# A recurrent attention and gated feed-forward kernel: chunk 0's keys and right side moved ahead of the first inverse, x kept in channel order, weights loaded into five rooms

## The chip, the cores and the metric

The kernel runs on one core of a Trainium2 chip. The metric is the device time of one execution in microseconds (us). The kernel before took 1059.27 us, the median of three runs (1058.33 to 1067.59). The profile is of one more execution, which took 1057.22 us.

The core's engines have their own instruction queues and run in order: TensorE (PE in the profile, its weight loads PEld) multiplies matrices into PSUM; VectorE (DVE), ScalarE (ACT) and GpSimd (POOL) work elementwise; SyncE (SP) only issues DMA transfers, and so does ScalarE at the start. In the profile SPq and ACTq are these issues.

## The reference

Two blocks, one behind the other. The first is a linear recurrence over 768 tokens for 4 batches and 8 heads of 40 channels, with a state of 40 x 40 per head:

```
for t in range(S):
    y[t]  = r[t] @ state
    Sa    = state @ a[t]
    state = state * w[t] - outer(Sa, b[t]) + outer(v[t], k[t])
```

`w` is a decay per channel, between 0.85 and 0.95. The heads of `y` side by side are `x`, 3072 tokens of 320 channels. The second block is a feed-forward layer with 2048 hidden channels:

```
h = x @ w_in
out = (h * sigmoid(h)) @ w_out
```

All inputs are float32 except the weights of the second block, which are float64 and come to the device as pairs of 32-bit words.

## The kernel before

**Chunks.** The sequence is cut into 12 chunks of 64 tokens (index n). A unit (n, m) is one chunk of two of the four batches with all their heads; a chunk has two units. Inside a chunk the recurrence becomes matrix products with a triangular matrix that has to be inverted. Two heads lie on the partitions, 64 apiece, of which 40 are used.

**Preparing a unit** (`pre`, `scale` and `scores`). VectorE scans the decays into their running products `W` (L229) and takes the reciprocal (L238); GpSimd scales `a` (L239) and the keys `kb` (L241). TensorE forms the scores (L209, in `between`), VectorE masks them (L217), and SP writes them to DRAM as `md` (L257). The tile of decays, `w0`, is one buffer; the load of the next unit's decays (`load_w`, L196) waits until the former unit is done with it. Only the first four units have a tile each (`w0` and `early`), loaded on ScalarE's queue.

**Inverting** (`inverse`). For two chunks at a time, 128 triangular blocks of 32 x 32 lie on the 128 partitions (`mi`, read back from `md`, L275). VectorE inverts them in `XI`, column by column, 31 rows of a product and a reduction each (L279, L285). Then `XI` goes to DRAM (`zd`, L292) and also turned (ScalarE's copy into `mi`, L293; `xd`, L294), and is fetched into `XT` (L307, L310). `merge` completes the 64 x 64 inverses with small products (L322, L339).

**The chain of a unit** (`chain`). `keys` transposes the keys (L385); `right` forms the right side from scores (L209, L217), from the carried state `Gbd` (L394) and from the values (L406) and copies it into `RHS`; `solve` applies the inverse (L428, L446); `update` brings the state forward (L466, L475, L479); `read` and `write` form the output (L505, L513, L525, L532, L543) and write it to DRAM as `xs` (L552 to L557); `turn` transposes the state for the next chunk (L488, L497).

**The gated part** (`moe`) takes the 512 tokens of two chunks at a time. `fetch` reads `xs` into `xt` (L569, L571). A part is 16 steps: four `first` (L581, L586, the sigmoid L589 and the product L590 into `gts`), four `second` (L597, L606), then four and four again with the other half of the hidden channels (L597, L609, and the output's transfer L613). `in_order` keeps its matmuls in the order of the program.

**Weights** (`weights`). The float64 weights are loaded in 40 pieces of 128 x 256 numbers, and each is converted to float32 by five VectorE and three ScalarE instructions (L147 to L155). A piece is loaded by up to four transfers (L142) right ahead of its conversion, into a tile that rotates through two or three others (`room`, `xt`, `mi`, `tmp`). `x` is held in an order of its own, three groups of 40 channels and eight more on 128 partitions, so the rows of `w_in` are picked to match.

**The order of work.** The program writes steps in an order made by hand; `weave` merges lists of steps evenly. A planner then orders each engine's queue by its own model of time, with the program's order as priority, so an instruction may run ahead of others that the program has before it, where its data and buffers allow. PSUM tiles named `att` (five) serve the attention, `moe` (three) the gated part. `tc.issue_after(x)` keeps instructions of the same engine behind the instruction x.

The program's order is: load four units, prepare chunk 0; prepare chunk 1, with the first four pieces of weights ahead of the inverse; the inverse; then for each chunk its loads, its chain, and the preparation of the chunk after the next. Pieces 4 to 19 are woven with chunk 0's chain, 20 to 35 with chunk 1's. The preparation of chunks 2 and 3, the second inverse and the last four pieces are woven with the first 12 steps of the first gated part:

```
if n == 1:
    queue = more
    fetch()
    with tc.issue_after(mark["turn"]):
        weave(queue[0:12], ready + held + ahead)
```

From chunk 2 on a chunk's chain is woven with up to eight gated steps; behind an odd chunk the fetch and four steps of the next gated part follow at once, so that an even chunk finds 12 steps in the queue and an odd one four.

A last check counts scan values beyond a limit; if any is, a slow path at the end computes all again. It doesn't run here.

## Time and profile before

| | |
|---|---|
| median of three runs | 1059.27 us |
| profiled execution | 1057.22 us |
| its span, first to last instruction | 1055.4 us |
| mean granted TensorE clock | 0.921 |
| TensorE busy | 847.7 us (80%) |
| VectorE busy | 575.7 us (55%) |
| ScalarE busy | 291.4 us (28%) |
| GpSimd busy | 92.9 us (9%) |
| bytes moved by DMA | 85.37 MB, 81 GB/s in the mean |

Busy time counts an engine's own instructions, not the issue of transfers. A group's row gives line, engine, operation, output and inputs, shapes and count, then busy time, mean duration in ns of one, idle time just before, and what ended it. A row of the timeline gives start, duration, engine, line, operation, output and inputs, count, and in brackets the idle time before it with what ended it. A stretch's row gives start and end, length, busy time and count of the engines named, the granted TensorE clock (1.00 is full), the share of the 16 DMA engines that was busy, and GB/s.

### The profile page before, as it was taken

Reading aid. Unit: us, or ns where it says so; the run is one execution under the profiler, and the core shown is the slowest. Engines: PE = TensorE matmul, PEld = TensorE weight load, DVE = VectorE, ACT = ScalarE, POOL = GpSimd, SP = SyncE. Lnnn points to the kernel's source line nnn. Section 1 sums busy time; section 2 is a strip of 40 time slices with the busy share of each in tenths; the row PEclk is TensorE's granted clock in tenths of the full one; section 3 lists DMA queues with packets and bytes.
Section 4 is the critical chain, followed back from the end, with each engine's and each line's share of the span. In section 5 each row is a group of like instructions: output and inputs, shape, how many; then the busy total and the mean of one; then the engine's idle time right before and its main releaser. Section 6 shows DMA issues by size and latency. Waiting matters only on the chain.

```text
span 1055.4 us, 25618 instructions
## 1 busy us (share of the span) xinstructions
PE 847.7 (80%) x11010; PEld 591.2 (56%) x11010; DVE 575.7 (55%) x1039; ACT 291.4 (28%) x628; POOL 92.9 (9%) x90
## 2 busy tenths in 40 slices
PE   0004899079979768999897999889999899996997
PEld 0003889025359662676663686735667647775444
DVE  8793474766942669525379345398164780412111
ACT  1303462642213321242212233122423023230110
POOL 6101000012000110000100002010001000000000
PEclk9999776579987887999899999989999999998999
DMA  6433353454033543333440343421433403202001
GB/s 155 127 80 80 91 142 95 132 145 97 10 92 82 131 105 56 77 83 85 98 124 12 71 121 88 109 76 44 88 92 78 119 15 69 60 21 56 0 1 28
DMA packets 200424, 85.37 MB, mean 81 GB/s; under 512 B 161648, under 2 KB 191856, under 8 KB 200304
## 3 DMA queue, kind: packets, MB, share of 16 engines
q1 hardware_dynamic: 197584, 83.01, 31.8%
q8 instruction: 88, 1.44, 0.6%
q10 hardware_dynamic: 2720, 0.66, 0.3%
q14 instruction: 32, 0.26, 0.1%
HBM read 66.32 MB, written 17.30 MB: 79 GB/s over the span
## 4 chain that ended last, share of the span: by engine, by line
PE 58%; DVE 24%; DMA 7%; SPq 3%; issue 3%; ACT 3%; POOL 2%; DVEq 0%; POOLq 0%; ACTq 0%
PE po L597 16%; PE ph L581 10%; DVE tmp L279 6%; DVE XI L285 5%; DVE w L238 5%; PE pl L505 4%; PE ph L586 3%; PE pm L209 3%; PE py L525 3%; PE pu L428 3%; PE py L532 3%; PE pt L385 2%; PE po L339 2%; PE pg L466 2%; PE pr L406 2%
## 5 line engine op out<-in xcount | busy, mean ns | idle before, releaser
L581 PE MATMUL ph<-xt,wi_s 128*128 128x512 f32 x384 | 197.4, 649 | 70.0 <-DMA xt<-xs 52.3
L597 PE MATMUL po<-wo_s,gts 128*128 128x320 f32 x768 | 219.9, 442 | 0.0
L597 PEld LDWEIGHTS po<-wo_s,gts 128*128 128x128 f32 x768 | 144.8, 193 | 64.3 <-issue 4.8
L581 PEld LDWEIGHTS ph<-xt,wi_s 128*128 128x128 f32 x384 | 72.4, 203 | 168.8 <-issue 70.3
L590 DVE TENSOR_TENSOR gts<-ph,sg 128x512 f32<-128x512 f32 x96 | 63.6, 683 | 153.5 <-ACT sg L589 153.4
L589 ACT ACTIVATE sg<-ph 128x512 f32<-128x512 f32 x96 | 52.6, 595 | 240.4 <-PE ph L586 240.3
L279 DVE TENSOR_TENSOR tmp<-XI,mi 128x1 f32<-128x1 f32 (+30 forms) x186 | 102.5, 551 | 8.8 <-DMA mi<-md 4.0
L285 DVE TENSOR_REDUCE XI<-tmp 128x1 f32<-128x1 f32 (+30 forms) x186 | 93.2, 501 | 5.2
L209 PE MATMUL pm<-a,kb 64*64 64x64 f32 x1536 | 48.1, 244 | 52.4 <-POOL kb L241 22.2
L322 PE MATMUL pq<-XT,sb 32*32 32x32 f32 x768 | 25.7, 199 | 69.9 <-DMA XT<-zd 69.9
L241 POOL TENSOR_TENSOR kb<-kb,w 128x512 f32<-128x512 f32 x42 | 50.8, 1231 | 320.7 <-DVE w L238 185.6
L209 PEld LDWEIGHTS pm<-a,kb 64*64 64x64 f32 x1536 | 38.8, 151 | 62.3 <-POOL kb L241 39.7
L238 DVE RECIPROCAL w<-W 128x512 f32<-128x512 f32 x21 | 70.3, 3349 | 1.3
L322 PEld LDWEIGHTS pq<-XT,sb 32*32 32x32 f32 x768 | 23.1, 115 | 76.8 <-issue 75.5
L217 DVE TENSOR_TENSOR sk<-pm,ms 128x256 f32<-128x256 f32 x48 | 18.1, 416 | 83.5 <-PE pm L209 83.1
L239 POOL TENSOR_TENSOR a<-a,W 128x512 f32<-128x512 f32 x24 | 28.2, 1178 | 395.2 <-DMA a<-in_aT 261.5
L586 PE MATMUL ph<-xt,wl_s 64*128 64x512 f32 x192 | 61.0, 671 | 0.0
L497 ACT COPY GT<-pt 40x512 f32<-40x512 f32 x44 | 25.5, 579 | 98.0 <-PE pt L488 97.3
L475 DVE TENSOR_TENSOR Gbd<-pg,Gbd 64x320 f32<-64x320 f32 x44 | 21.5, 488 | 52.0 <-PE pg L466 51.2
L543 DVE TENSOR_TENSOR yx<-py,W 64x512 f32<-64x512 f32 x48 | 33.0, 688 | 30.1 <-PE py L532 29.4
L505 PE MATMUL pl<-r,vut 64*128 64x64 f32 x768 | 49.4, 285 | 0.0
L505 PEld LDWEIGHTS pl<-r,vut 64*128 64x128 f32 x768 | 47.8, 200 | 1.7 <-issue 1.2
(98 smaller groups left out, 1023.7 us busy)
## 6 DMA issues: line engine op xcount, KB each, us to landing
a<-in_aT SPq DMA_DIRECT2D x24, 256.0 KB
kb<-in_bT SPq DMA_DIRECT2D x48, 128.0 KB
kb<-in_kT SPq DMA_DIRECT2D x48, 128.0 KB
vut<-in_vT SPq DMA_DIRECT2D x48, 128.0 KB
r<-in_rT SPq DMA_DIRECT2D x24, 256.0 KB
room<-in_w_out SPq DMA_DIRECT2D x20, 256.0 KB
room<-in_w_in SPq DMA_DIRECT2D x48, 80.0 KB
v<-in_v SPq DMA_DIRECT2D x48, 80.0 KB
```

The costliest lines, as they stand in the source:

```text
L209: nc.tensor.matmul(pm[j][C * be : C * be + C, p * C : p * C + C], lhsT=u.kb[J, q, n, :], rhs=u.a[J, q, :], start=True, stop=True,)
L238: nc.vector.reciprocal(R, u.W[:, :, 1 : C + 1])
L241: nc.gpsimd.tensor_tensor(out=u.kb[:, :, n], in0=u.kb[:, :, n], in1=R, op=ALU.mult)
L279: nc.vector.tensor_tensor(out=tmp[:, 0:n, 0:n], in0=XI[:, t + 1 : 32, t + 1 : 32], in1=mi[:, t, t + 1 : 32].unsqueeze(1).to_broadcast([128 ...
L285: last = nc.vector.tensor_reduce(out=XI[:, t + 1 : 32, t], in_=tmp[:, 0:n, 0:n], axis=AX.X, op=ALU.add)
L322: nc.tensor.matmul(pq[be][r + 32 : r + 64, h * 32 : h * 32 + 32], lhsT=s[r : r + 32, h, 32:64], rhs=X[r : r + 32, h, 32:64], start=True, s ...
L505: nc.tensor.matmul(pl[j][:, q * C : q * C + C], lhsT=u.vut[J, q].rearrange("p n t -> p (n t)"), rhs=u.r[J, q, :], start=True, stop=True,)
L581: in_order(nc.tensor.matmul(ph[n], lhsT=wi_s[:, k, at : at + 128], rhs=xt[:, k, :], start=k == 0, stop=False))
L586: in_order(nc.tensor.matmul(ph[n], lhsT=wl_s[R, i, :], rhs=xt[R, 2, :], start=False, stop=True))
L589: nc.scalar.activation(out=sg, in_=ph[n], func=AF.Sigmoid)
L590: nc.vector.tensor_tensor(out=box["gts"][:, (2 * i + n) % (NF // 2), :], in0=ph[n], in1=sg, op=ALU.mult)
L597: in_order(nc.tensor.matmul(po[:, 0:DM], lhsT=box["gts"][:, f, b * 128 : b * 128 + 128], rhs=wo_s[:, NF // 2 * half + f, :], start=f == 0, ...
```

## The change

- Chunk 0's values and queries are loaded with the first units, and its `keys` and `right` stand ahead of the first inverse. In chunk 0 the products with the state, which is zero there (L394 and L525), are left out.
- The first eight pieces of weights are converted between the start of the first inverse and its rows. What follows, the loads of chunk 2 included, is traced behind the last row (VectorE instructions only behind that row). The preparation of chunk 2 moves from there into chunk 1's chain, that of chunk 3 and the second inverse stay with the first gated part.
- The loads of weights are parted from the conversions: five are issued at the start, into four rooms laid in the tile `gts` and one `room`, and each conversion issues the load five pieces on. In the second half there are three rooms (`room`, `mi`, `tmp`) and the load is three pieces on. Pieces 8 to 19 are woven with chunk 0, 20 to 33 with chunk 1, 34 to 39 with the first gated part.
- `x` is held in channel order: `xs` is two writes per unit instead of six, a piece of `w_in` is one transfer (the pieces of the last 64 rows are two).
- A unit's decays are two transfers over all 128 partitions instead of four; the padding's zeros need ones in `one`, and the memset of the whole tile goes.
- The turned copy of `XI` is split between ScalarE and VectorE.
- Gated steps: none with chunks 2 and 3, eight with each chunk from 4 on; none placed behind an odd chunk but the fetch. Four steps of the gated part before are left in the queue ahead of each new one, also at the end.

```diff
     early = [
         sb.tile([128, 32 * 32], F32, name=x)[:, 0 : Q * (C + 1)].rearrange("p (q t) -> p q t", q=Q)
-        for x in ("tmp", "mi", "room")
+        for x in ("tmp", "mi", "xt")
     ]
+    for w in [w0] + early:
+        nc.vector.memset(w[:, :, 0:1], 0.0)
     nc.vector.memset(one, 0.0)
+    for j in range(2):
+        nc.vector.memset(one[DP * j + 32 : DP * j + DP], 1.0)
+        nc.vector.memset(one[DP * j + 32 : DP * j + D], 0.0)
     nc.vector.memset(one[:, :, 0:1], 1.0)
-    for w in [w0] + early:
-        nc.vector.memset(w, 1.0)
-        nc.vector.memset(w[:, :, 0:1], 0.0)
...
+    def load_weights(n):
+
+        if n == 0:
+            rooms["gts"] = sb.tile([128, 4, 4 * WS], I32, name="room4", tag="gts")
+        if n < NW // 2 and n % 5 < 4:
+            rooms[n] = rooms["gts"][:, n % 5]
+        else:
+            tag = "room" if n < NW // 2 else ("room", "mi", "tmp")[n % 3]
+            rooms[n] = sb.tile([128, 4 * WS], I32, name="room", tag=tag)
+        for lo, hi, src in pieces[n][1]:
+            raw = rooms[n][lo:hi, 0 : 2 * WS]
+            nc.sync.dma_start(raw.rearrange("p (i x) -> p i x", x=256) if len(src.shape) == 3 else raw, src)
...
         nc.vector.tensor_tensor(out=dst, in0=f, in1=e, op=ALU.mult)
+        ahead = 5 if n + 5 < NW // 2 else 3
+        if n + ahead < NW and (n + 5 < NW // 2 or n + ahead >= NW // 2):
+            load_weights(n + ahead)
...
         for be in range(2):
-            for j in range(2):
-                J = slice(DP * j, DP * j + D)
-                queue.dma_start(
-                    at[J, P * be : P * be + P, 1 : C + 1],
-                    wT[2 * u.m + be, u.n, J].rearrange("p (q t) -> p q t", q=P),
-                )
+            queue.dma_start(
+                at[:, P * be : P * be + P, 1 : C + 1], wT[2 * u.m + be, u.n].rearrange("p (q t) -> p q t", q=P)
+            )
...
             nc.sync.dma_start(zd, XI)
-            nc.scalar.copy(out=mi, in_=XI.rearrange("p t s -> p s t"))
+            turned = XI.rearrange("p t s -> p s t")
+            nc.scalar.copy(out=mi[:, 0:16], in_=turned[:, 0:16])
+            nc.vector.tensor_copy(out=mi[:, 16:32], in_=turned[:, 16:32])
             nc.sync.dma_start(xd, mi)
...
-            for p in range(P):
+
+            for p in range(P if u.n > 0 else 0):
...
-            for q in range(Q):
+            for q in range(Q if u.n > 0 else 0):
...
             for j in range(2):
                 nc.sync.dma_start(
-                    x[0 : 3 * D, j].rearrange("(p e) t -> e p t", p=3), y[DP * j : DP * j + D, 0:3]
-                )
-                nc.sync.dma_start(x[3 * D : 128, j], y[8 * j : 8 * j + 8, 3])
-            nc.sync.dma_start(x[0:24, 2], y[16:D, 3])
-            nc.sync.dma_start(x[24:64, 2], y[DP : DP + D, 3])
+                    xs[:, at : at + 2 * C].rearrange("(p two e) t -> two e p t", two=2, e=D)[j],
+                    y[DP * j : DP * j + D],
+                )
...
+    for n in range(5):
+        load_weights(n)
+    convert = [partial(weights, n) for n in range(NW)]
+    xs = dr.tile([DM, 4 * NM * C], F32, name="xs", bufs=2)
+    for u in units[0]:
+        load_rv(u)
+    run(prepare(0))
     for t in RHS + Gbd + GT + XT:
         nc.gpsimd.memset(t, 0.0)
...
+    run(prepare(1))
+    chains = {0: [chain(u, xs) for u in units[0]]}
+    run([x[i] for i in range(2) for x in chains[0]])
+    steps = invert(1)
+    run(steps[0:1] + convert[0:8] + steps[1:32])
     queue = []
...
+    with tc.issue_after(mark["row"]):
+        for u in units[2]:
+            load(u)
+        run(steps[32:])
+        steps = [x for pair in zip(*[x[2:] for x in chains[0]]) for x in pair]
+        weave(late.pop(0) + steps, convert[8:20])
+        for u in units[1]:
+            load_rv(u)
+        for u in units[3]:
+            load(u)
+        steps = [x for pair in zip(*[chain(u, xs) for u in units[1]]) for x in pair]
+        weave(steps[0:4], convert[20:24])
+        weave(steps[4:], convert[24:34], prepare(2))
+    fetch, queue = moe(0, xs)
+    fetch()
+    with tc.issue_after(mark["turn"]):
+        weave(queue[0:12], prepare(3) + convert[34:] + invert(3))
+    del queue[0:12]
+    for n in range(2, NN):
...
+        now = 8 if n > 3 else 0
+        weave(steps[0:4], queue[0 : now // 4])
+        weave(steps[4:], queue[now // 4 : now], prepare(n + 2) + invert(n + 2))
+        del queue[0:now]
         if n % 2 == 1:
             fetch, more = moe(n // 2, xs)
...
+            fetch()
+            queue += more
+    run(queue)
```

`prepare(n)` now holds only the preparation, `invert(n)` the inverse and the merges; `run` executes a list of steps. The slow path at the end follows the new order of `x`.

90 lines of the change are left out of this document (24 added, 66 removed).

## The prediction

> **What bounds the kernel now.** I read busy time by stretch first, cut where the chain of waits changes hands, then the timeline at the cuts. Columns: microseconds, length, then PE (TensorE), its weight loads, DVE (VectorE), ACT (ScalarE) and POOL with instruction counts, granted clock, DMA share, GB/s.
>
> ```profile
> span 1055.4 us, 25618 instructions
> ```
>
> ```profile
> 16.00:20.00 4.00, 0.60 (x24) 0.41 (x16) 3.95 (x5) 3.38 (x7) 4.00 (x5) 1.00 0.90 208
> 34.10:46.60 12.50, 0.00 (x0) 0.00 (x0) 7.74 (x17) 4.85 (x13) 0.00 (x0) 1.00 0.51 143
> 46.60:86.50 39.90, 0.00 (x0) 0.00 (x0) 37.97 (x71) 3.56 (x9) 5.75 (x4) 1.00 0.33 83
> 86.50:115.20 28.70, 19.72 (x432) 18.60 (x432) 4.53 (x14) 10.87 (x19) 2.35 (x2) 0.97 0.45 115
> 115.20:184.60 69.40, 64.82 (x1106) 61.44 (x1105) 41.78 (x111) 32.01 (x78) 0.00 (x0) 0.69 0.40 108
> 184.60:214.70 30.10, 1.00 (x35) 0.73 (x32) 23.57 (x76) 18.69 (x46) 0.00 (x0) 0.57 0.51 152
> 214.70:308.30 93.60, 80.86 (x289) 41.08 (x290) 70.87 (x119) 24.99 (x52) 11.65 (x10) 0.94 0.32 78
> 540.60:595.50 54.90, 46.93 (x200) 24.89 (x199) 46.02 (x69) 13.14 (x25) 4.87 (x4) 0.97 0.23 62
> 682.20:738.20 56.00, 50.74 (x259) 28.31 (x258) 49.60 (x81) 12.82 (x24) 4.87 (x4) 0.94 0.22 63
> 974.10:1055.40 81.30, 73.72 (x224) 38.74 (x224) 12.27 (x20) 10.40 (x20) 0.00 (x0) 0.96 0.04 9
> ```
>
> There are two regimes. Up to 86.5 us TensorE waits for the first inverse, and VectorE is the engine at work (37.97 of 39.90). From 308 us on TensorE is fed, with holes in the windows where a later inverse runs (8.0 of 54.9 and 5.3 of 56.0 us idle in the two shown). Between lies the costliest hole, 184.6 to 214.7: one TensorE microsecond in thirty, while VectorE and ScalarE convert weights. The last stretch is one whole gated part, its 16 steps in 73.7 us of TensorE. So a microsecond saved ahead of 308 us is worth about one at the end; later only holes count.
>
> The sum is made against the profiled execution: 1057.2 us, of which 1055.4 are span. The median of the three runs, 1059.3, is 2 us above it.
>
> **Start and first inverse.**
>
> ```profile
> 2.03 3.84 ACTq L196 DMA_DIRECT2D w<-in_wT  x4
> ```
>
> ```profile
> 8.54 1.24 DVE L229 TENSOR_TENSOR_SCAN W<-w,one 128x520 f32<-128x520 f32 x1 [3.57 <-DMA w<-in_wT]
> ```
>
> ```profile
> 32.24 1.23 DVE L229 TENSOR_TENSOR_SCAN W<-w,one 128x520 f32<-128x520 f32 x1
> 33.60 3.35 DVE L238 RECIPROCAL w<-W 128x512 f32<-128x512 f32 x1
> ```
>
> ```profile
> L217 DVE TENSOR_TENSOR sk<-pm,ms 128x256 f32<-128x256 f32 x48 | 18.1, 416 | 83.5 <-PE pm L209 83.1
> ```
>
> VectorE's share of the rows' stretch, 46.5 to 86.5 us:
>
> ```profile
> L279 DVE TENSOR_TENSOR tmp<-XI,mi 128x1 f32<-128x1 f32 (+30 forms) x31 | 16.9, 546 | 0.9
> L285 DVE TENSOR_REDUCE XI<-tmp 128x1 f32<-128x1 f32 (+30 forms) x31 | 15.6, 502 | 1.0
> L238 DVE RECIPROCAL w<-W 128x512 f32<-128x512 f32 x1 | 3.3, 3343 | 0.0
> L229 DVE TENSOR_TENSOR_SCAN W<-w,one 128x520 f32<-128x520 f32 x1 | 1.2, 1230 | 0.0
> ```
>
> Work on the tile room alone (VectorE, ScalarE, POOL):
>
> ```profile
> 115.20:184.60 69.40, 23.20 (x75) 18.20 (x45) 0.00 (x0) 0.69 0.40 108
> 184.60:214.70 30.10, 22.30 (x72) 17.63 (x44) 0.00 (x0) 0.57 0.51 152
> ```
>
> Five VectorE instructions make a piece: 75 are 15 pieces, 1.55 us of VectorE each. Where conversions run alone, 14.4 pieces in 30.1 us, a piece takes 2.1.
>
> (a) The first decay load is two transfers instead of four, and waits for no memset of the whole tile. Four issues took 3.84 us, the scan began 2.7 us behind the last. Two are worth at most 1.9, the memset 1.0. Padding adds bytes while the transfer engines are 0.90 busy, which could take all of it. I take 2: VectorE is done with its four units, and free, near 30 instead of 32.2.
>
> (b) Then come four score masks of chunk 0 (1.7) and eight conversions instead of four: 8 x 1.55 to 2.1, so rows start between 44 and 49. I take 47, no gain: the four extra conversions fill the wait in which VectorE now idles (12.50 less 7.74) and the scan and reciprocal at 32.24, 4.6 us, which leave. Ahead of the score writes the queue now gets, by the shapes in the code, 1.31 MB of weights, 1.66 MB of values and queries, and 0.4 MB of padding: 3.4 MB at 208 GB/s are 16 us, from 20 to 36. The scores, written and read back behind them, then land near 41, hidden by the conversions up to 47. With that cover gone I allow 6 us.
>
> (c) The rows' stretch loses a scan and reciprocal (4.5) and a conversion (1.55): 39.9 becomes 33.8, end near 81. Gain 6.
>
> (d) Behind the rows:
>
> ```profile
> 86.52 1.96 ACT L293 COPY mi<-XI 128x1024 f32<-128x1024 f32 x1 [1.99 <-DVE XI L285]
> ```
>
> ```profile
> 88.09 0.76 SPq L196 DMA_DIRECT2D w<-in_wT  x1
> 88.95 0.44 SPq L292 DMA_DIRECT2D zd<-XI  x1
> ```
>
> ```profile
> 94.37 0.81 PE L322 MATMUL pq<-XT,sb 32*32 32x32 f32 x12 [62.86 <-DMA XT<-zd]
> ```
>
> The first write back waited 2.4 us behind decay loads that aren't there any more, and half of the turned copy goes to VectorE: ScalarE's 1.96 becomes about 1.0. TensorE starts 6 us behind the rows instead of 7.9, at 87 instead of 94.4.
>
> (e) Keys and right side of chunk 0, in TensorE's groups from 94.3 to 115.3 us:
>
> ```profile
> L385 PE MATMUL pt<-ident,kb 128*128 128x128 f32 x16 | 3.7, 424 | 0.0
> L406 PE MATMUL pr<-v,sk 64*64 64x40 f32 x64 | 2.6, 228 | 0.0
> L209 PE MATMUL pm<-a,kb 64*64 64x64 f32 x64 | 2.4, 272 | 0.0
> L394 PE MATMUL pr<-Gbd,a 128*64 128x80 f32 x32 | 2.0, 266 | 0.0
> ```
>
> Of 10.7 us 2.0 are dropped, and 8.7 move to where TensorE is idle. Some overlapped the merge; I take 9. The first solve moves from 115 to 98.
>
> **Chunks 0 and 1** (115.2 to 184.6). TensorE loses half of this group, 5 us:
>
> ```profile
> L525 PE MATMUL py<-r,GT 64*64 64x64 f32 x128 | 10.4, 278 | 2.7 <-DVE Gbd L475 2.6
> ```
>
> VectorE gains: 26 pieces instead of 15 (+17) and the two units of chunk 2 (+9). Loads of five pieces lie ready when the rows end, and from 81 to 98 VectorE has little else (4.53 of 28.70 now), so 8 pieces fall there (-12). 41.8 + 17 + 9 - 12 = 56 us of VectorE stand beside 60 of TensorE, in a chain that alternates between them. I take 66 for 69.4, bounds 60 and 82: end at 164.
>
> **The hole in front of the gated part.**
>
> ```profile
> 164.06 26.00 SPq L142 DMA_DIRECT2D room<-in_w_in  x19
> ```
>
> ```profile
> 202.38 0.36 SPq L552 DMA_DIRECT2D xs<-yx  x1
> ```
>
> ```profile
> 214.72 6.00 PE L581 MATMUL ph<-xt,wi_s 128*128 128x512 f32 x8 [28.90 <-DMA xt<-xs]
> ```
>
> From 164 us SP's queue holds weight loads, each waiting for a room that a conversion must empty, so x, computed by 184, was written at 202. In the changed kernel six pieces come behind chunk 1 instead of twenty, a w_in piece is one transfer instead of four, and x is two writes per unit instead of six. What is left is the round trip; a later one took 8.3 us, from 540.6 to this row:
>
> ```profile
> 548.87 3.70 PE L581 MATMUL ph<-xt,wi_s 128*128 128x512 f32 x8 [2.32 <-DMA xt<-xs]
> ```
>
> I take 12 for 30.1: the gated part starts at 176 instead of 214.7.
>
> **To the merge of chunk 2.**
>
> ```profile
> 239.66 1.23 DVE L229 TENSOR_TENSOR_SCAN W<-w,one 128x520 f32<-128x520 f32 x1
> ```
>
> ```profile
> 285.82 17.61 PE L597 MATMUL po<-wo_s,gts 128*128 128x320 f32 x64
> 308.29 0.92 PE L322 MATMUL pq<-XT,sb 32*32 32x32 f32 x14 [4.86 <-DMA XT<-zd]
> ```
>
> Chunk 3's second unit is scaled 25 us behind the gated part's start; the second inverse follows, and the merge at 308. The 16 gated steps need 74 us, VectorE's share is 70.87, little changed. I take 85 for 93.6: 261 instead of 308. Running sum -47.
>
> **The rest.** Chunk 2 loses its four steps of filler. Just these (17.61 us above) run ahead of the merge now, though the program has them behind it; they can do so again, and I cost it at nothing. If they can't, a rival below has the price. In three later windows the four leftover steps stand in front of the fetch of x and cover it: -4 each. At the end TensorE waits for the last fetch:
>
> ```profile
> 974.08 5.21 PE L581 MATMUL ph<-xt,wi_s 128*128 128x512 f32 x8 [8.69 <-DMA xt<-xs]
> ```
>
> Four leftover steps take that place: -9. Fewer issues on SP, of a third to one microsecond each by the rows above, in chunks 2 and 3: -3. In all -47 - 12 - 9 - 3 = -71; 1057.2 - 71 = 986.
>
> **Rivals.**
>
> The queue holds x again. Loads are now issued right behind a conversion, a round ahead, and so stand even earlier in SP's queue. For it: the row at 164.06. Against: six pieces are left, not twenty. It costs the 18 us from 184 to 202, and some 6 more for chunk 3's decay loads in the same queue: 1010.
>
> Full clock in chunks 0 and 1. If feeding TensorE without gaps lifted 0.69 to the next gated stretch's 0.94, its 60 us would be 44 and VectorE's 56 decide: 10 less, 976. Against: TensorE was busy 93% there, and got 0.69. [...]
>
> No change that can be measured. VectorE's work ahead of the second merge isn't smaller: 186 busy us between 34 and 308 (six rows above), 68%. If waits keep that density, nothing is gained there and the end's 9 us are left: 1048.
>
> Slower: the inverse windows run dry. Now four gated steps and a fetch are placed at the window itself. In the changed kernel none is; all must come forward past the merge. If they can't, a window of 55 us has no matmul, 47 more idle than now, at four windows (behind chunks 3, 5, 7, 9): +188, against -59 from the rest, 1186. It decides from 15 us more per window. Against: 285.82, where four steps did come forward.
>
> Early transfers that crowd the score writes are inside the range, by (b). [...]
>
> **How the numbers follow.** Forecast, 986: 0.62. Queue: 0.16. Full clock: 0.06. No change: 0.08. Dry windows: 0.08. The forecast's own range is 973 to 1009, its bounds added as squares: start (-3, +6), chunks 0 and 1 (-6, +16), the stretch to 308 between 74 and 94 (-11, +9), windows without gain (+12). Below, the range reaches on to the full clock with all lower bounds (976 - 20), above to the queue's 1010 with the windows and the stretch to 308 at their upper ends (+21): 956 to 1031. About 1% is what a measurement of this kernel tells from no change. Faster: 0.62 + 0.16 + 0.06 = 0.84; same 0.08; slower 0.08.
>
> **What would show it.** Rows in one piece of 34 us that ends near 81, with no scan in it; first pq near 87; keys and right side ahead of 50. Chunk 1's last yx near 164, xs and xt directly behind, ph near 176. The next merge's pq near 261. No idle in front of the last gated part. It is wrong if the rows start behind 55, if weight loads stand between yx and xs, or if the windows behind chunks 5 and 7 show over 10 us idle.

## The result, and the profile after

The changed kernel took 979.44 us, the median of four runs (971.43 to 991.06), against 1058.8 for the kernel before beside it: a ratio of 0.922, with a 95% interval of 0.912 to 0.932. In a second group of runs it took 974.74 (972.2 to 976.51), a ratio of 0.915 (0.910 to 0.920). The profile of the first group was of a disturbed execution, so the lines here are from the second, which took 972.2 us. Against the 1057.2 of the profile before these are 85 us less; 71 were forecast.

The stage marks of the two profiles, in us from the start of the span:

| mark | before | forecast | after |
|---|---|---|---|
| first row of the first inverse | 46.6 | 47 | 46.3 |
| last row ends | 86.5 | 81 | 83.5 |
| first pq (merge of chunk 0) | 94.4 | 87 | 89.3 |
| first solve (pu) | 115.2 | 98 | 106.1 |
| last x of chunk 1 computed | 183.5 | 164 | 173.4 |
| first gated matmul (ph) | 214.7 | 176 | 179.4 |
| merge of chunk 2 (pq) | 308.3 | 261 | 265.9 |
| merge of chunk 4 | 443.2 | | 397.7 |
| merge of chunk 6 | 595.4 | | 529.9 |
| last matmul ends | 1047.8 | | 963.0 |

42 us are gained up to the merge of chunk 2 (47 forecast), 42 behind it (24 forecast).

Busy time by stretch of the changed kernel, cut at or near these marks; the columns are those of the prediction's first fence (engines with instruction counts, granted clock, DMA share, GB/s):

```profile
28.00:39.00 11.00, 7.70 (x176) 6.99 (x176) 10.39 (x31) 8.00 (x21) 1.45 (x2) 0.97 0.57 118
39.00:46.30 7.30, 0.00 (x0) 0.00 (x0) 0.02 (x1) 0.24 (x1) 0.00 (x0) 0.50 0.75 181
46.30:83.50 37.20, 0.00 (x0) 0.00 (x0) 35.27 (x78) 5.41 (x14) 0.00 (x0) 0.50 0.49 124
89.30:106.10 16.80, 13.22 (x256) 12.91 (x256) 10.53 (x18) 7.53 (x17) 3.88 (x3) 0.50 0.49 117
106.10:172.70 66.60, 62.84 (x1064) 60.19 (x1063) 50.88 (x119) 34.19 (x87) 3.73 (x3) 0.71 0.53 142
172.70:179.40 6.70, 0.60 (x15) 0.44 (x12) 6.46 (x19) 4.25 (x10) 0.00 (x0) 0.66 0.63 182
179.40:265.90 86.50, 74.62 (x269) 36.96 (x270) 74.33 (x125) 24.93 (x56) 12.14 (x10) 0.91 0.22 57
397.70:529.90 132.20, 127.35 (x1842) 88.59 (x1841) 85.43 (x139) 38.77 (x84) 14.40 (x12) 0.99 0.41 97
```

The keys and right side lie in the first stretch, where TensorE was idle before. The hole ahead of the gated part, 30.1 us long before, is 6.7; counted from the end of the last x it was 31.2 and is 6.0. From the merge of chunk 4 to that of chunk 6 it takes 132.2 us instead of 152.2.

The second line is not what was forecast: ahead of the first row VectorE has nothing to do for 7.3 us. The timeline there (start, duration, engine, line, operation; in brackets the idle time in front and what ended it):

```profile
30.52 9.07 SPq L264 DMA_DIRECT2D md<-sb  x16
39.69 1.27 SPq L204 DMA_DIRECT2D w<-in_wT  x2
41.08 1.23 SPq L282 DMA_DIRECT2D mi<-md  x2
42.36 3.92 SPq L145 DMA_DIRECT2D room<-in_w_in  x6
46.30 0.16 DVE L286 TENSOR_TENSOR tmp<-XI,mi 128x1 f32<-128x1 f32 x1 [7.28 <-DMA mi<-md]
```

Only five of the eight conversions were done at 39, those whose pieces were loaded at the start. SP took 9.07 us to issue 16 writes of the scores, then loaded decays, then read the scores back; the loads of the next pieces stood behind that, at 42.4. So the other three conversions came between the first rows, from 47.2 to 52.3.

The merge of chunk 0, on ScalarE (`qq` is the copy of the first product `pq`, which the second product `po` needs):

```profile
92.19 0.58 ACT L341 COPY qq<-pq 32x512 f32<-32x512 f32 x1
96.82 0.63 ACT L251 ACTIVATE junk<-w 128x512 bf16<-128x512 f32 x1 [4.05 <-DVE w L245]
97.56 0.58 ACT L341 COPY qq<-pq 32x512 f32<-32x512 f32 x1
```

and on TensorE:

```profile
98.19 1.00 PE L348 MATMUL po<-XT,qq 32*32 32x32 f32 x15 [3.46 <-ACT qq L341]
```

Between the two copies that the merge waits for, ScalarE's queue holds a sum of squares of chunk 2's decays, which waits for VectorE's reciprocal of them. So the scaling that the rows got rid of stands in the merge now.

### The profile page after: what moved, and what is told of

It is laid out like the page before. It is cut to its first block, busy times and chain, and to the rows that moved or that the text cites. A ratio compares the mean times of both kernels' runs of the same rounds, so it can differ in the third digit from the quotient of the medians.

```text
span 989.2 us, 25109 instructions
## 1 busy us (share of the span) xinstructions
PE 849.9 (86%) x10914; PEld 597.4 (60%) x10914; DVE 581.3 (59%) x1045; ACT 281.1 (28%) x628; POOL 92.9 (9%) x90
## 5 line engine op out<-in xcount | busy, mean ns | idle before, releaser
L605 PE MATMUL po<-wo_s,gts 128*128 128x320 f32 x768 | 214.5, 436 | 0.0
L589 PEld LDWEIGHTS ph<-xt,wi_s 128*128 128x128 f32 x384 | 70.2, 198 | 124.1 <-issue 65.7
L286 DVE TENSOR_TENSOR tmp<-XI,mi 128x1 f32<-128x1 f32 (+30 forms) x186 | 100.0, 537 | 11.0 <-DMA mi<-md 6.0
L216 PE MATMUL pm<-a,kb 64*64 64x64 f32 x1536 | 45.7, 240 | 39.5 <-POOL kb L248 20.6
L216 PEld LDWEIGHTS pm<-a,kb 64*64 64x64 f32 x1536 | 36.8, 148 | 50.8 <-POOL kb L248 41.0
L515 PE MATMUL pl<-r,vut 64*128 64x64 f32 x768 | 60.6, 310 | 0.0
L515 PEld LDWEIGHTS pl<-r,vut 64*128 64x128 f32 x768 | 58.8, 223 | 1.6 <-issue 0.9
L594 PE MATMUL ph<-xt,wl_s 64*128 64x512 f32 x192 | 58.0, 671 | 0.5 <-DMA xt<-xs 0.5
L485 DVE TENSOR_TENSOR Gbd<-pg,Gbd 64x320 f32<-64x320 f32 x44 | 21.5, 488 | 57.4 <-PE pg L476 56.4
```

The lines of the kernel that those rows point to most:

```text
L216: nc.tensor.matmul(pm[j][C * be : C * be + C, p * C : p * C + C], lhsT=u.kb[J, q, n, :], rhs=u.a[J, q, :], start=True, stop=True,)
L286: nc.vector.tensor_tensor(out=tmp[:, 0:n, 0:n], in0=XI[:, t + 1 : 32, t + 1 : 32], in1=mi[:, t, t + 1 : 32].unsqueeze(1).to_broadcast([128 ...
L515: nc.tensor.matmul(pl[j][:, q * C : q * C + C], lhsT=u.vut[J, q].rearrange("p n t -> p (n t)"), rhs=u.r[J, q, :], start=True, stop=True,)
L589: in_order(nc.tensor.matmul(ph[n], lhsT=wi_s[:, k, at : at + 128], rhs=xt[:, k, :], start=k == 0, stop=False))
L594: in_order(nc.tensor.matmul(ph[n], lhsT=wl_s[R, i, :], rhs=xt[R, 2, :], start=False, stop=True))
L605: in_order(nc.tensor.matmul(po[:, 0:DM], lhsT=box["gts"][:, f, b * 128 : b * 128 + 128], rhs=wo_s[:, NF // 2 * half + f, :], start=f == 0, ...
```

## The experiments

Each is the changed kernel with one edit, unless it says otherwise. They ran in three groups, each beside the kernel before: medians 1063.7 (first four), 1062.3 (next four) and 1057.7 (last four). Across groups the ratios are compared.

**The changed kernel again** (no edit).

> The changed kernel once more, unchanged, for a profile beside the others on one chip. Both theories: 970 to 985 us, second merge's first pq between 262 and 275 us.

Measured: 974.74 us, ratio 0.915 (0.910 to 0.920).

**Only the placement of the gated steps**, put into the kernel before.

```
-            weave(steps[0:4], queue[0:2])
-            weave(steps[4:], queue[2:8], ahead)
-            del queue[0:8]
+            now = 8 if n > 3 else 0
+            weave(steps[0:4], queue[0 : now // 4])
+            weave(steps[4:], queue[now // 4 : now], ahead)
+            del queue[0:now]
...
-                left = max(...)
-                queue[left:left] = [fetch]
+                fetch()
                 queue += more
-                take = len(queue) - 12 if n + 2 < NN else 0
-                weave(queue[0:take])
-                del queue[0:take]
```

> The kernel before with only the new placement of the gated steps (none with chunks 2 and 3, eight with each chunk from 4 on, none behind an odd chunk, four left in the queue). Theory of the prediction, in which this part is worth 12 us in the windows and 9 at the end: 1036 us. Rival, in which the windows are the larger half of the gain: 1015 to 1025 us. Rival of the dry windows: slower than before.

Measured: 1037.4 us (1025.56 to 1044.19), ratio 0.967 (0.958 to 0.977): 26 us less than the kernel before beside it by the medians, 35 by the ratio.

**Only that placement undone** in the changed kernel (the same lines the other way round).

> The changed kernel with the old placement of the gated steps, all else kept. Theory of the prediction: 21 us slower than the changed kernel, about 997 us. Rival (windows are the larger half): 35 us or more slower, 1010 us or above. Dry windows: faster than the changed kernel.

Measured: 1002.04 us (998.94 to 1015.05), ratio 0.944 (0.936 to 0.952): 27 more than the changed kernel by the medians, 31 by the ratios. The two chunks from the merge of chunk 4 on, with the placement undone:

```profile
397.00:544.00 147.00, 137.88 (x1863) 93.59 (x1862) 86.06 (x139) 39.28 (x85) 14.00 (x12) 0.97 0.36 87
```

and those of the kernel before with the new placement:

```profile
446.50:586.60 140.10, 132.58 (x1838) 90.68 (x1838) 86.22 (x138) 40.13 (x84) 13.99 (x12) 0.96 0.38 89
```

132.2 became 147.0; 152.2 became 140.1. Done alone and undone alone, the placement is worth 26 and 27 us by the medians, 35 and 31 by the ratios; the forecast had 21 (three windows of 4 and the end's 9). The windows did not run dry.

**Chunk 0's keys and right side behind the inverse again.**

```
-    run([x[i] for i in range(2) for x in chains[0]])
...
-        steps = [x for pair in zip(*[x[2:] for x in chains[0]]) for x in pair]
-        weave(late.pop(0) + steps, convert[8:20])
+        steps = [x for pair in zip(*chains[0]) for x in pair]
+        steps[4:4] = late.pop(0)
+        weave(steps, convert[8:20])
```

> The changed kernel with chunk 0's keys and right side behind the inverse again (still without the products with the zero state). Theory of the prediction: their 8 us come back onto the path, 984 us. Rival, in which the merge, not they, sets the first solve, as copies on ScalarE leave TensorE time for them: no more than 3 us slower, 979 us.

Measured: 992.86 us (988.4 to 994.49), ratio 0.930 (0.924 to 0.935): 18 more, beyond both expectations. From the first pq to the first solve it takes 24.4 us (87.9 to 112.4) instead of 16.8, close to the 8 expected; as the rows ended 1.5 us earlier, only 6 of the 18 are at the first solve. The others arise in chunks 0 and 1 and in front of the gated part; this run's stretches:

```profile
32.00:87.90 55.90, 0.00 (x0) 0.00 (x0) 45.82 (x114) 11.59 (x28) 0.00 (x0) 1.00 0.41 106
87.90:108.00 20.10, 15.56 (x336) 14.57 (x336) 9.20 (x18) 9.42 (x21) 3.55 (x3) 1.00 0.30 57
112.40:190.00 77.60, 68.42 (x1073) 64.68 (x1072) 50.93 (x125) 36.12 (x91) 3.50 (x3) 0.70 0.52 137
190.00:201.80 11.80, 0.00 (x0) 0.00 (x0) 10.39 (x26) 5.81 (x15) 1.14 (x1) 0.50 0.86 219
```

Chunks 0 and 1 take 77.6 us instead of 66.6 with the same VectorE work (50.93 and 50.88), and the hole is 11.8 instead of 6.7. Which wait makes the 11 us was not tried. The wait of the merge for chunk 2's reciprocal is here as well:

```profile
95.34 0.63 ACT L251 ACTIVATE junk<-w 128x512 bf16<-128x512 f32 x1 [4.04 <-DVE w L245]
```

**Chunk 2's scaling behind the merge.**

```
             for g, J in halves:
-                nc.vector.tensor_tensor(
+                last = nc.vector.tensor_tensor(
                     out=g, in0=g, in1=u.W[J, :, C : C + 1].to_broadcast([DP, Q, D]), op=ALU.mult
                 )
+            if u.n == 0:
+                mark["update"] = last.ins
...
-        weave(steps[4:], convert[24:34], prepare(2))
+        weave(steps[4:], convert[24:34])
+        with tc.issue_after(mark["update"]):
+            run(prepare(2))
```

> The changed kernel, with the scaling of chunk 2's two units (scan, reciprocal, their squares on ScalarE) held back until chunk 0's state update is done. Theory: in the merge of chunk 0 ScalarE waited 4.05 us for chunk 2's reciprocal ahead of the second qq copy, and TensorE waited for that copy 3.5 us; with the scaling behind the merge the first solve starts at 101 to 102.5 instead of 106.1, and the kernel takes 970 to 972 (3 to 5 less), since the 4.6 us of VectorE's scan and reciprocal that leave come back where VectorE has some slack. Rival A: the merge is slow because its matmuls run at half clock; then the first solve stays above 105 and the time at 974 to 976. Rival B: the scaling comes too late for chunk 2, whose scores then hold up the second inverse: first solve at 102, but 980 or more.

Measured: 982.64 us (973.87 to 992.52), ratio 0.925 (0.915 to 0.935): not faster than the changed kernel. The merge, on ScalarE:

```profile
91.92 0.58 ACT L341 COPY qq<-pq 32x512 f32<-32x512 f32 x1
92.79 0.58 ACT L341 COPY qq<-pq 32x512 f32<-32x512 f32 x1 [0.30 <-PE pq L331]
```

and where the saved time went, on VectorE and TensorE:

```profile
101.98 1.61 PE L438 MATMUL pu<-RHS,XT 64*64 64x40 f32 x26
221.14 0.16 DVE L286 TENSOR_TENSOR tmp<-XI,mi 128x1 f32<-128x1 f32 x1 [6.33 <-DMA mi<-md]
272.47 1.19 PE L331 MATMUL pq<-XT,sb 32*32 32x32 f32 x32
```

The two copies follow each other, the first solve comes at 102.0 and the gated part at 172.1, 7 us earlier. So the reciprocal did cost the merge 4 us; the granted clock was 0.50 in this merge as in the changed kernel's. But chunk 2's scaling comes later (its second scan at 172.1 instead of 133.6), chunk 3's with it (195.9 instead of 192.7), the second inverse waits for the scores, begins at 221.1 instead of 212.9, and the merge of chunk 2 stands 6.6 us later. That was rival B's mechanism.

**Two places for the weights**, each piece loaded right ahead of its conversion.

```
-        if n == 0:
-            rooms["gts"] = sb.tile([128, 4, 4 * WS], I32, name="room4", tag="gts")
-        if n < NW // 2 and n % 5 < 4:
-            rooms[n] = rooms["gts"][:, n % 5]
-        else:
-            tag = "room" if n < NW // 2 else ("room", "mi", "tmp")[n % 3]
-            rooms[n] = sb.tile([128, 4 * WS], I32, name="room", tag=tag)
+        tag = ("room", "xt")[n % 2] if n < NW // 2 else ("room", "mi", "tmp")[n % 3]
+        rooms[n] = sb.tile([128, 4 * WS], I32, name="room", tag=tag)
...
     def weights(n):
+        load_weights(n)
...
-    for n in range(5):
-        load_weights(n)
...
```

> The changed kernel, with every weight piece loaded right ahead of its conversion as before: two places in turn for the first half, three for the second, no load a round ahead. Theory: the loads that lie ready let eight conversions fill the wait for the scores and more of them the stretch behind the rows; with two places each conversion waits for a transfer of about 3 us and the loads stand in SP's queue in front of the scores' and x's transfers. Rows start 5 or more us later, the gated part starts at 187 or later instead of 179.5, and the kernel takes 985 to 1000 (10 to 25 more). Rival: conversions are limited by VectorE and not by places: the gated part starts by 182 and the kernel takes at most 978.

Measured: 980.47 us (975.49 to 984.57), ratio 0.925 (0.917 to 0.933), less than the 985 to 1000 of the theory. The rows began 4.8 us earlier, not 5 later:

```profile
25.63 8.83 SPq L257 DMA_DIRECT2D md<-sb  x16
41.46 0.16 DVE L279 TENSOR_TENSOR tmp<-XI,mi 128x1 f32<-128x1 f32 x1 [5.44 <-DMA mi<-md]
```

Without weight loads in front of them on SP the 16 writes were issued from 25.6 on instead of 30.5. All conversions then came behind the start of the rows, which ended at 85.1 instead of 83.5. The 3 us of transfer ahead of each conversion were the author's estimate; VectorE's conversions waited for a load seven times in the first 330 us, 0.4 to 2.2 us each. The gated part starts at 188.5, 9 us later, but the merge of chunk 2 at 269.0, only 3 later. Five places are worth 6 us by the medians and 11 by the ratios; the intervals overlap, so neither is clear of noise.

**x in the old order of channels.**

```
-                pieces.append((wi_s[:, k, c : c + WS], [(0, 128, w_in[128 * k : 128 * k + 128, 2 * c : 2 * (c + WS)])]))
+                parts = [(D * i, D * i + D, w_in[D * (2 * i + k) : D * (2 * i + k) + D, X2]) for i in range(3)]
+                parts.append((3 * D, 128, w_in[spare + 8 * k : spare + 8 * k + 8, X2]))
+                pieces.append((wi_s[:, k, c : c + WS], parts))
...
             for j in range(2):
-                nc.sync.dma_start(
-                    xs[:, at : at + 2 * C].rearrange("(p two e) t -> two e p t", two=2, e=D)[j],
-                    y[DP * j : DP * j + D],
-                )
+                nc.sync.dma_start(
+                    x[0 : 3 * D, j].rearrange("(p e) t -> e p t", p=3), y[DP * j : DP * j + D, 0:3]
+                )
+                nc.sync.dma_start(x[3 * D : 128, j], y[8 * j : 8 * j + 8, 3])
+            nc.sync.dma_start(x[0:24, 2], y[16:D, 3])
+            nc.sync.dma_start(x[24:64, 2], y[DP : DP + D, 3])
...
```

> The changed kernel, with x in the old order of channels: a piece of the first weight matrix is four transfers instead of one, x of a unit is written in six transfers instead of two. Theory (the sum's size): 3 us in chunks 2 and 3 by SP's issues, and a few us in front of the first gated part (the second transfer of x later by 4 issues): 980 to 984, gated part at 182 to 184. Rival A: what remains of the gain behind the merge of chunk 2 beside the placement of the gated steps (16 us between two earlier runs) is due to these transfers: then it takes 990 to 995, with intervals between the merges of the pairs 4 to 6 us longer each. Rival B: SP has room for all of them: 973 to 977.

Measured: 999.88 us (997.57 to 1007.94), ratio 0.945 (0.937 to 0.953): 25 us more than the changed kernel by the medians, 32 by the ratios, and the largest single part beside the placement; rival A had named these transfers, with 990 to 995. 6 us stand at the merge of chunk 2 (272.1 for 265.9), 19 behind it. Its two chunks from the merge of chunk 4 on:

```profile
405.70:544.40 138.70, 130.61 (x1840) 88.84 (x1840) 85.30 (x139) 39.21 (x84) 14.53 (x12) 0.99 0.39 93
```

138.7 for 132.2, and 139.4 for 132.1 in the next two (1.8 and 2.9 us more in the pairs before and behind). TensorE is idle 8.1 us there instead of 4.9, and busy 3.3 us more with as many matmuls. Its waits over these two pairs of chunks (us in total, times, longest), first the changed kernel's:

```profile
PE ph L589 <- DVE gts L598: 6.4, 4, 2.6
```

then with the old order:

```profile
PE ph L595 <- DVE gts L604: 10.8, 4, 5.4
```

So 4.4 of 13.8 us are gated matmuls that wait for VectorE, which is at the inverse's rows. How more transfers lead there, and where the other 9 us arise, stays open; the planner puts the gated steps elsewhere once the transfers are other ones, and the runs don't separate that from SP's time.

**Eight writes of the scores instead of 16** for the first inverse.

```
-            M = slice(u.m, u.m + 1) if u.n < 2 else slice(0, NM)
-            for be in range(2 if u.n < 2 or u.m == NM - 1 else 0):
+            M = slice(0, NM)
+            for be in range(2 if u.m == NM - 1 else 0):
```

> The changed kernel, with the scores of chunks 0 and 1 written for both units at once: 8 writes in place of 16. Theory: rows start when SP has issued the 16 writes (9.07 us, from 30.5 to 39.7), the next decay load and the read back; half as many writes take about 4.5 us, so rows start at 42 to 43 instead of 46.3, the first solve comes 3 to 4 us earlier and the kernel takes 970 to 972. Rival A: the transfers and not the issues set the time (the engines are 0.85 to 0.89 busy from 40 to 60 us): rows still start at 46 and the time stays at 974 to 976. Rival B: rows start earlier but conversions, loads or the merge give it back: rows at 42 to 43, time at 974 to 976.

Measured: 970.85 us (968.65 to 989.64), ratio 0.916 (0.908 to 0.923), no different from the changed kernel's. The start moved as expected:

```profile
29.92 4.32 SPq L264 DMA_DIRECT2D md<-sb  x8
41.54 0.16 DVE L286 TENSOR_TENSOR tmp<-XI,mi 128x1 f32<-128x1 f32 x1 [2.20 <-DMA mi<-md]
101.34 1.61 PE L438 MATMUL pu<-RHS,XT 64*64 64x40 f32 x26
```

Half the writes, with the same bytes (8 of 64 KB for 16 of 32), took 4.32 us, the rows began 4.8 us earlier and so did the first solve; the run with both edits, below, has the same two marks (41.5 and 101.3). From the end of the read back's issue to the first row it took about as long as before, 3.7 us for 4.0. So SP's issues set the start of the rows, as the run with two places shows too, where the same 16 writes began 4.9 us earlier.

**Chunk 3's scaling and scores not held** until chunk 1's state is turned.

```
-        weave(steps[4:], convert[24:34], prepare(2))
+        weave(steps[4:], convert[24:34], prepare(2) + prepare(3))
...
-        weave(queue[0:12], prepare(3) + convert[34:] + invert(3))
+        weave(queue[0:12], convert[34:] + invert(3))
```

> The changed kernel, with chunk 3's scaling and scores no longer held until chunk 1's states have been turned: they are woven into chunk 1, behind chunk 2's. Theory: the merge of chunk 2 is set by VectorE and not by the gated steps: chunk 3's two scalings (scans at 178 and 193 in the profile of the changed kernel), then the second inverse's rows from 213, 20 us behind the second of them, 45 us of rows, 7 us to the merge at 266. With the hold gone the scans come at about 165 and 180, rows start at 203 to 207 (the last conversion bounds them), the merge comes at 257 to 260 and the kernel takes 966 to 970 (5 to 9 less). Rival A: VectorE has no room: what is scaled earlier pushes conversions and x of chunk 1 back by as much, the gated part starts 5 or more us later and the merge stays at 264 to 268: 973 to 977. Rival B: the gated steps bound it: the merge stays although rows end earlier.

Measured: 970.71 us (967.22 to 974.8), ratio 0.923 (0.914 to 0.932), not separated from the changed kernel (0.915).

```profile
212.61 0.37 DVE L161 TENSOR_TENSOR wo_s<-room 128x256 f32<-128x256 f32 x1
212.88 1.14 DVE L286 TENSOR_TENSOR tmp<-XI,mi 128x1 f32<-128x1 f32 x1
260.55 1.19 PE L331 MATMUL pq<-XT,sb 32*32 32x32 f32 x32
```

Half of each story. Chunk 3 was scaled by 182 instead of 193, but the last conversion moved from 206.8 to 212.6 and the rows began directly behind it, at 212.9 as in the changed kernel. The gated part started 11 us later, at 190.6; the merge of chunk 2 came 5 us earlier all the same. VectorE has hardly a gap in front of these rows (14.17 of the 14.9 us ahead of them are busy), so what goes first pushes the rest back; and the gated part's start doesn't set the merge. The 5 us lie inside the rows: in the changed kernel a scan of chunk 4's decays and its reciprocal stand among them, at 217.5, with a wait of 2.2 us for the decays in front; here both units of chunk 4 are scaled before the first row.

**Both of the last two edits.**

> Both of the edits that have a theory behind them: chunk 3's scaling not held, and the scores of chunks 0 and 1 in 8 writes instead of 16 (rows started at 41.5 instead of 46.3 there). Theory: the two add: rows at 41.5, the first solve at 101, the merge of chunk 2 at 252 to 256, the kernel 961 to 966. Rival: 4 to 5 us saved ahead are lost again by VectorE's queue or by a lower granted clock in the first 300 us, as with the 8 writes alone: 968 to 975.

Measured: 969.58 us (965.3 to 984.35), ratio 0.921 (0.910 to 0.932). The marks add as expected (first solve 101.3, merge of chunk 2 at 255.5, last matmul's end 956.1 for 963.0), but the ratio does not separate it from the changed kernel.

**28 more matmuls on TensorE while VectorE computes the rows.**

```
+    dummy = moe_bank("dummy")
+    for i in range(28):
+        nc.tensor.matmul(
+            dummy, lhsT=ident, rhs=units[0][1].kt.rearrange("p q e -> p (q e)")[:, 0:512], start=True, stop=True
+        )
     steps = invert(1)
```

> The changed kernel with 28 more matmuls of 128x128x512 on TensorE behind chunk 0's right side, while VectorE computes the rows; nothing reads their result, and the output is the same. In the changed kernel the granted clock falls to 0.50 at 39, some 10 us after keys and right side start, and stays there through the idle time and the merge until about 110. Theory A: the clock falls after a stretch of dense matmuls and comes back about 20 us of busy time later, whatever it is busy with; with the extra matmuls (21 us at full, 42 at half clock) it is back to 1.00 by the merge, the first solve comes at 101 to 104, and chunks 0 and 1 end 2 to 5 us earlier: 970 to 973. Theory B (idle time in front halves the clock, a few busy us restore it): 1.00 within 5 us of the first extra matmul and through the merge as well. Rival C: small matmuls don't care for the clock, since other waits set their pace: the clock is at 1.00 in the merge and the times stay as they are, 973 to 976.

Measured: 972.42 us (970.27 to 987.91), ratio 0.922 (0.910 to 0.933); the first solve at 106.2. This run's stretches:

```profile
56.00:62.00 6.00, 5.81 (x14) 2.28 (x12) 5.55 (x14) 0.00 (x0) 0.00 (x0) 1.00 0.86 217
62.00:66.00 4.00, 0.00 (x0) 0.00 (x0) 3.79 (x7) 0.00 (x0) 0.00 (x0) 0.87 0.77 174
66.00:88.00 22.00, 0.00 (x0) 0.00 (x0) 21.27 (x34) 3.34 (x7) 0.00 (x0) 0.50 0.23 74
88.00:112.00 24.00, 19.16 (x394) 18.75 (x396) 12.80 (x29) 12.22 (x28) 3.88 (x3) 0.50 0.47 114
```

The last 50 of the extra matmuls' 56 instructions took 21.73 us and ended at 62, with the granted clock at 1.00; in the 4 idle us behind them it was 0.87, in the 22 behind those 0.50: none of the three theories as written. A has the fall behind dense work, and these 22 us of it ran at 1.00. B's fall and rise stand in the kernel before, where the clock was 0.50 from 190 to 210, without a matmul, 0.53 from 210 to 220, in which the gated part starts, and 1.00 from 220 to 230. Here it fell in idle time too, but 19 busy us in the 24 behind 88 ran at 0.50.

**Chunk 2's loads and first scaling ahead of the rows again.**

```
-    run(steps[0:1] + convert[0:8] + steps[1:32])
+    run(steps[0:1] + convert[0:8])
+    for u in units[2]:
+        load(u)
+    scaled = prepare(2)
+    run(steps[1:16] + scaled[0:2] + steps[16:32])
...
-        weave(steps[4:], convert[24:34], prepare(2))
+        weave(steps[4:], convert[24:34], scaled[2:])
```

> The changed kernel, with chunk 2's loads, the scan and reciprocal of its first unit and that unit's scores moved ahead of the rows again, as the kernel before had one of these units there. Theory (the prediction's part c): VectorE's scan and reciprocal, 4.6 us, stand in front of the rows or in them; rows end 3 to 5 us later, the first solve comes 0 to 5 us later (the merge no longer waits for this reciprocal, 4 us), 974 to 979. Rival: they fall into the 7.3 us in which VectorE waits for the scores before the first row, and cost nothing there; then the first solve comes at 102 and the kernel takes 970 to 972.

Measured: 967.99 us (961.18 to 973.88), ratio 0.919 (0.907 to 0.930), no slower than the changed kernel.

```profile
42.09 1.24 DVE L236 TENSOR_TENSOR_SCAN W<-w,one 128x520 f32<-128x520 f32 x1 [3.02 <-DMA w<-in_wT]
43.43 3.35 DVE L245 RECIPROCAL w<-W 128x512 f32<-128x512 f32 x1
47.04 0.15 DVE L286 TENSOR_TENSOR tmp<-XI,mi 128x1 f32<-128x1 f32 x1
99.32 0.63 ACT L251 ACTIVATE junk<-w 128x512 bf16<-128x512 f32 x1 [4.05 <-DVE w L245]
```

Scan and reciprocal fell into the wait for the scores, and the first row came 0.7 us later, as the rival said. The merge got no faster: now the second unit's reciprocal stands in it, with the same 4.05 us. So the rival's first solve at 102 didn't come, it came at 108.6; the merge of chunk 2 came at 256.6.

## Why the prediction was right, and where not

The time, 986 forecast, 979 and 975 measured, was inside the range. The mechanism of most terms held, but the total came out better than its parts: up to the first solve 9 us were gained for 17 forecast, in chunks 0 and 1 and the hole 26 for 21.5, up to the merge of chunk 2 7 for 9, behind it 42 for 24. That these misses partly cancel is luck. The steps, by their own terms:

(a) Held. The first scan began at 6.70 instead of 8.54, 1.8 earlier for the 2 taken.

(b) The number held (46.3 for 47), its reason failed. Eight conversions were to hide the scores' way until 47; five were done at 39, three had no data yet, and the scores, to "land near 41", took until 46.3. The mis-sized term is the issue of 16 writes, 9.07 us, which the prediction did not cost. With eight, the rows began at 41.5.

(c) Mis-sized: the rows took 37.2 us for 33.8 (39.9 before). 78 VectorE instructions stand there, 62 of them rows; 15 of the others are the three conversions whose loads came behind the score writes, and at 1.55 us each, the prediction's price, they are more than the miss. A gain of 3 for the 6 forecast, the rows' end at 83.5 for 81.

(d) Held: the first pq 5.8 us behind the rows (6 forecast).

(e) The step that failed most in the head. The merge to the first solve was to take 11 us and took 16.8. Chunk 2's scaling, now behind the rows, stood in the merge, and its reciprocal held ScalarE 4.05 us between the two copies; held back, the merge took 12.9 (89.1 to 102.0). It isn't the absence of the keys that let it in: with the keys behind the inverse the same wait took 4.04. The other 2 us of the miss stay open. The prediction had noted that scan and reciprocal leave the rows, but not where they arrive.

Chunks 0 and 1: 66.6 for 66 at a cut of 172.7, where the last x isn't quite done. From the first solve to the last x it was 68.3 us and is 67.3, so 1 is gained for 3.4 forecast. The hole: 6.7 for 12, 6.0 from the last x, and the gated part at 179.4 for 176. Of the rivals, the queue did not hold x again: its last unit was written and fetched between 170 and 179.

To the merge of chunk 2: 86.5 for 85, right in size and wrong in its cause. The prediction counted 85 us from the gated part's start. The runs show that the start doesn't set it:

| run | gated part starts | chunk 3's second scan | last conversion | second inverse's rows begin | a scan of chunk 4 among the rows | merge of chunk 2 |
|---|---|---|---|---|---|---|
| changed kernel | 179.4 | 192.7 | 206.8 | 212.9 | yes | 265.9 |
| chunk 2's scaling behind the merge | 172.1 | 195.9 | 206.8 | 221.1 | yes | 272.5 |
| old order of channels | 196.7 | 199.3 | 213.0 | 217.7 | yes | 272.1 |
| keys and right side behind | 201.8 | 209.7 | 219.1 | 232.5 | yes | 283.2 |
| 28 more matmuls | 180.8 | 194.2 | 208.3 | 214.4 | yes | 267.8 |
| two places | 188.5 | 192.0 | 217.2 | 222.2 | no | 269.0 |
| chunk 3 not held | 190.6 | 181.7 | 212.6 | 212.9 | no | 260.6 |
| the same, eight writes | 185.1 | 176.2 | 207.4 | 207.7 | no | 255.5 |
| chunk 2's first scaling ahead | 186.5 | 194.3 | 205.6 | 211.1 | no | 256.6 |

The gated part that starts first has one of the latest merges. The merge stands 51 to 54 us behind the second inverse's first row where a scan of chunk 4 stands among the rows, and 45 to 48 where none does. The rows begin behind the last conversion, by 0.3 to 14 us; in two runs they wait for the scores (6.33 us with chunk 2's scaling held, 3.86 with the keys behind), in the changed kernel chunk 4's first reciprocal and products of the gated part stand in front of them. So what VectorE has in its queue ahead of these rows and among them sets this merge. The rival "no change" had said as much: VectorE's work up to the merge isn't smaller, and if its density stays, nothing is gained. The work did stay, and the density did not. The changed kernel, and then the kernel before:

```profile
34.00:265.90 231.90, 154.33 (x1693) 113.28 (x1694) 188.14 (x390) 84.02 (x202) 19.74 (x16) 0.73 0.42 109
```

```profile
34.00:308.30 274.30, 166.40 (x1857) 121.86 (x1858) 186.55 (x403) 94.97 (x215) 19.76 (x16) 0.85 0.38 101
```

188 of 232 us (81%) against 187 of 274 (68%). The gain of the head is VectorE's waits, 44 us of 88 gone. Whether the other 44 can go is not shown.

The rest: 24 forecast, 42 measured, the largest miss. Two terms were mis-sized. The placement of the gated steps (windows of 4 each and the end's 9) measured 26 to 27 by the medians instead of 21. Fewer issues on SP, "of a third to one microsecond each", were costed at 3 us in chunks 2 and 3 alone; the order of channels measured 19 behind the merge of chunk 2, in every pair of chunks. The prediction priced these issues by their own duration and only in two chunks; why the order of channels is worth as much as it is in the later pairs stays open. The two together (26 + 19 = 45) come near the 42, though how far they overlap was not tried.

The prediction also counted idle time alone. From the merge of chunk 2 to the last matmul, the kernel before and then the changed one:

```profile
308.30:1047.80 739.50, 676.76 (x9026) 465.54 (x9026) 361.82 (x602) 189.39 (x396) 52.09 (x44) 0.94 0.30 72
265.90:963.00 697.10, 665.65 (x9047) 459.64 (x9046) 363.53 (x608) 184.27 (x396) 52.51 (x44) 0.98 0.33 79
```

TensorE is idle 31.4 us there instead of 62.7, and its waits for x went from 23.4 us in five to 6.2 in one, 17 of the 21 that the windows and the end were to give; with the placement undone they are 17.5 in five again. The other 11 us are busy time: nearly the same matmuls took less of it, at a granted clock of 0.98 instead of 0.94. No term of the prediction had that, and what raised the clock was not tried.

Full clock in chunks 0 and 1: 0.71 in these 66.6 us, 0.69 before. The rival did not come.

Undone one at a time, the placement (27), the order of channels (25), the keys' place (18) and the five places (6) make 76 us by the medians, of the 89 between the two kernels in one group. The decays in two transfers, the split copy and the products left out were not undone alone.

## What to carry to other kernels

If a moved step frees an engine, look for what the planner or the queue puts into the gap, and at whose queue that stands in: here a reciprocal that left the rows came back in the merge, in front of a copy on another engine. Before a stretch is costed from the start of the stage that fills it, ask which engine's total work fits into it; a start that moves by 30 us over nine runs while the end follows another engine is that engine's stretch. And add up the issues of small transfers that stand on one queue in front of something awaited: 16 writes and the loads ahead of them held a read back, and with it the first inverse.

## What the hardware showed that was not expected

The granted clock. In the changed kernel it was 0.50 behind chunk 0's right side, from 39 on, through the idle rows and through the merge, was back at 0.95 between 110 and 133, and was 0.50 again in the 31 us behind that, in which TensorE had no gap:

```profile
39.00:89.00 50.00, 0.00 (x0) 0.00 (x0) 40.69 (x98) 9.59 (x24) 0.00 (x0) 0.50 0.56 148
89.00:110.00 21.00, 17.12 (x347) 16.82 (x347) 11.43 (x22) 10.28 (x23) 3.88 (x3) 0.50 0.50 121
110.00:133.00 23.00, 19.30 (x426) 17.86 (x424) 20.41 (x54) 14.12 (x36) 0.00 (x0) 0.95 0.56 143
133.00:164.00 31.00, 31.00 (x387) 30.20 (x386) 23.35 (x50) 15.06 (x41) 3.73 (x3) 0.50 0.51 139
```

With the extra matmuls it was 1.00 until 62, then 0.87 and 0.50 in the idle time; but with the keys and right side behind the inverse it was 1.00 in 55.9 idle us, and in the 20.1 of the merge behind them. So 31 us busy without a gap ran at 0.50, and 55.9 idle ones at 1.00: what sets the clock was not shown. The smallest matmuls were hardly slower at 0.50: the merge's 128 `pq` (32 x 32) took 236 ns each there, and 214 at 1.00 with the keys behind; its 128 `po` took 237 in both. The merge as a whole was not run at full clock with nothing else changed.

VectorE beside GpSimd. Of four like instructions of two conversions, the two that ran beside GpSimd's scaling of the keys took over four times as long (the fourth, L154 at 99.55, took 0.28 like the third):

```profile
96.98 1.27 DVE L153 TENSOR_SCALAR room<-room 128x256 int32<-128x256 int32 x1
98.16 1.26 DVE L154 TENSOR_SCALAR room<-room 128x256 int32<-128x256 int32 x1
99.34 0.28 DVE L153 TENSOR_SCALAR room<-room 128x256 int32<-128x256 int32 x1
```

```profile
96.86 2.41 POOL L248 TENSOR_TENSOR kb<-kb,w 128x512 f32<-128x512 f32 x2 [2.30 <-DVE w L245]
```

GpSimd's two instructions took 2.41 us, about 1.2 each, and the two of VectorE beside them 1.27 and 1.26. What holds VectorE's there was not shown. It is 2 us in this merge, with nothing waiting for those conversions.
